# Batch 2's input stage partly by seven block products, with sums moved between VectorE and GpSimd and a reordered lead-in and last tile

## The chip, the cores and the metric

The kernel runs on one core of a Trainium2 chip. A core has TensorE (PE, matrix products), VectorE (DVE), ScalarE (ACT), GpSimd (POOL) and SyncE (SP), which run side by side and wait for one another through semaphores. SBUF is the memory on the core, PSUM the eight banks that PE writes its products to. The metric is the device time of one execution in microseconds (us). Times are medians of several runs; a profile is one profiled execution, whose time is a little different.

## The reference

Sparse attention over four batches, eight heads, 768 positions of 64 values, followed by a feed-forward layer. Each query sees the keys within 15 positions, and a summary of each block of 32 keys: the maximum of the block's keys, and the mean of its values, with log(32) added to the score.

```python
k_sum = k.reshape(B, H, nb, block, D).max(axis=3)
v_sum = v.reshape(B, H, nb, block, D).mean(axis=3)
scores_l = where(abs(pos_q - pos_k) < 16, scale * q @ k.T, -1e9)
scores_s = scale * q @ k_sum.T + np.log(32)
a = softmax(concat(scores_l, scores_s))
x = (a @ concat(v, v_sum)).transpose(0, 2, 1, 3).reshape(3072, 512)
h = x @ w_in                                 # 512 -> 2048
g = h * (1.0 / (1.0 + np.exp(-1.702 * h)))   # gelu
out = g @ w_out                              # 2048 -> 512
```

## The kernel before, in words

**Stages.** The four batches run one behind the other, each with an input stage (x times w_in, then the gelu on ACT into `gT`) and an output stage (gT times w_out). Attention of batch b+1 runs in small pieces beside batch b's output stage. A lead-in (0 to about 20.5 us in the trace) makes the attention of batch 0's first half before anything else can run; there `idle(n)` issues n matmuls of no use that keep PE busy. Batch 2's input stage lies at 120.9 to 142.4 us, its output stage at 142.4 to 164.9, batch 3's input stage at 164.9 to 183 and its output stage to 202.4.

**Order.** There is no scheduler: every engine executes its instructions in the order in which the program issues them (`_Ordered`), so an instruction that waits holds up all behind it on its engine. Pieces of attention are put between the products by tables: `plan` maps a slot (the number of the product behind which they come) to pieces: `s` scores of a head pair (PE, then the exponential on ACT), `m` masks (DVE, `a_sb` times `mk`), `v` values (PE into `ps_av`, then on DVE the reciprocal `rc` and the norm), `d` the transposing DMA into x, `g` the loading of the gelu's table. The two digits are the half of the batch and the index; m12, for instance, is the mask of half 1, head pair 2, and v10 the values of half 1, first group.

**Input stage.** w_in has 16 tiles of 128 columns and a batch two halves of 384 rows. Plainly, each tile and half takes four matmuls of 384 columns (tile `ph`), then a gelu. Tiles j and j+8 make a pair. From batch 1 on, the output stage uses seven block products in place of eight (in the manner of Strassen), which needs sums of gelu outputs, `gs`, made by `g_sums(j)` for each pair, four sums each. Batch 3's input stage does the same for six of its eight pairs: `ff_product(j, n)` is product n of pair j, two matmuls each; 14 matmuls for a pair instead of 16. It needs sums of w_in's quarters, `wsi` (`win_sum(0..3)`, each an operation of 128 x 2048 on DVE, at the start of batch 2's input stage), and sums of x, `xs` (`x_sums`). Between the products of a pair stand copies of partial results: "a" (DVE, bank A to bank C), "s" (ACT, bank E to SBUF), "b" (DVE, A plus s into B), "c" (DVE, A plus s into E), and gelus from the banks C, B, E and A. `steps` gives the slot of each. For this the PSUM banks are divided into A (3), B (1), C (2) and E (2) by `last_bank`. In the other stages PSUM is a pool of four single banks (`pmm`, tag mm) and one of two double banks (`psb`, tag big).

**Beside the input stages** the keys and values of the batch after next are prepared: `value_rows` sums each block of v on PE (`vsum`, tile `ps_vs`), adds the two halves on DVE (`block_sums`: a copy to `vpart`, then four adds to `vs`) and spreads them by DMA; `rest_k` takes the block maxima of the keys (a reduction on DVE to `ks`) and copies them to their places in `kx`.

**Output stage.** For each row tile t of three, seven products of eight matmuls of 256 columns (`product(b, t, what)`, banks poA, poB, poC), in the order of `seq`; outputs are put together on DVE (`osb` = bank plus s1, s2 or s5) and by ACT, and are stored from SP's queue.

In the profile every instruction has line 28, that of the helper which keeps the order; instructions are told apart by their tiles. The names of tiles are kept when their memory is used again: the weight sums appear as writes to `kx` and `qT`, the x sums as writes to `vw`.

Of the kernel before, what the change touches and what calls it, by code (L numbers as in the profile page):

```python
# [9 lines left out]
F32 = mybir.dt.float32  # L10
# [25 lines left out]
def kernel(  # L36
# [308 lines left out]

    def flat_kx(p, s):
        return kx[p][s].rearrange("p t c -> p (t c)")

    def key_rows(p, s, ks, eng=dve, j0=0):
        flat = flat_kx(p, s)  # L350
# [225 lines left out]
                     in_=qb2[g].rearrange("p i a h d -> p (i a h d)"), transpose=True)  # L576

    def rest_k(p, s, eng=dve):
        ks = attp.tile([128, nb], BF16, name="ks", tag="ks")
# [21 lines left out]
    def values(b, half, g):  # L601
# [7 lines left out]
        for i in range(2):  # L609
# [4 lines left out]
            for hh in range(2):  # L614
                for j in range(JH):
                    for e in range(2):
# [2 lines left out]
                                  rhs=vw[b % 2][:, half * TH + t, p + hh * NP if b else 2 * p + hh, 0:D + 1],  # L619
                                  start=True, stop=True, skip_group_check=True)  # L620
        x2[g] = attp.tile([128, 2, JH, 2, D], F16, name="x2", tag="x2", bufs=4)
        for i in range(2):
            norm(x2[g][:, :, :, i].rearrange("p h j d -> p j h d") if b else x2[g][:, i], pvs[i])

    def norm(x, pv):
        rc = attp.tile([128, 2, JH, 1], F32, name="rc", tag="rc")
# [53 lines left out]
        gelu(half, nt, ph)  # L680


    def g_sums(j, eng=dve, which=(0, 1, 2, 3)):

        a1, a2 = gTb[:, j], gTb[:, j + NT // 2]
        l, r = slice(0, HALF), slice(HALF, S)
        for w in which:
            a, b_, op = {0: (a1[:, r], a2[:, r], ALU.add), 1: (gs[:, 0, j], a1[:, l], ALU.subtract),
                         2: (a1[:, l], a1[:, r], ALU.subtract), 3: (a2[:, l], gs[:, 1, j], ALU.subtract)}[w]
            eng.tensor_tensor(out=gs[:, w, j], in0=a, in1=b_, op=op)  # L690

    N1 = d_model // 2

# [22 lines left out]
    def win_sum(what):  # L716
# [6 lines left out]
        dve.tensor_tensor(out=wsi[what], in0=a, in1=b_, op=op)  # L723

    def x_sums():

# [3 lines left out]

    plast = {}

    def last_bank(tag, name):
        return plast[tag in "AB"].tile([128, 512], F32, name=name, tag="last" + tag,
                                       bufs={"A": 3, "E": 2, "B": 1, "C": 2}[tag])

    ff_now = {}

# [36 lines left out]
    def product(b, t, what):  # L775
# [30 lines left out]
        def give(o, cols, name):  # L806
# [4 lines left out]
            else:  # L811
                act.activation(out=now[t, o][:, cols], in_=po, func=ACT.Copy)

        def store(o, tok, cols=slice(0, d_model)):
            r0 = b * S + tok
            sp.dma_start(out=out[r0:r0 + 128, cols], in_=now[t, o][:, cols])
            if cols.start == 0:
                now.pop((t, o))

        last = b == B - 1 and t == JH - 1  # L820

        if what == 1:
            keep_it("s1")
        elif what == 2:
            give("o1", lo, "s1")
        elif what == 6:
            keep_it("s2")
        elif what == 5:
            keep_it("s5")
        elif what == 7:  # L830
            give("o2", hi, "s5")
            if last:
                store("o2", HALF + t * 128, hi)
        elif what == 3:
            give("o1", hi, "s2")
            store("o1", t * 128)
        else:
            give("o2", lo, None)
            store("o2", HALF + t * 128, lo if last else slice(0, d_model))

    seq = [(0, 1)]
    for t in range(JH):
# [129 lines left out]
    av_blocks(1)  # L972
    v_norm(0)
# [139 lines left out]


    halves[0] = True
    for b in range(1, B - 1):
        nxt = b + 1 < B
        s = (b + 1) % 2
        if b == B - 2:
            for w in range(4):  # L1120
                win_sum(w)
        for n in range(0, NT, 2):
            if n == 0:
                ff_open(order2[0:4], (lambda: tx(1, 1)) if b == 1 else None)
            elif n == 2:
                for nt in order2[0:4]:
                    ff_one(1, nt)
                g_sums(0)
                g_sums(1)
            else:  # L1130
                for nt in order2[n:n + 2]:
                    for half in range(2):
                        ff_one(half, nt)
                g_sums(n // 2, dve, (0, 1) if n + 2 == NT else (0, 1, 2, 3))
            if nxt:
                if n == 0 and b > 1:
                    pool.tensor_copy(out=gate2, in_=xTT[1][1][:, 1, 0:1])
                    load_turned(q, b + 1, qb2, "qb")
                if n // 2 == 1:
                    value_rows(s)  # L1140
                if n // 2 == 2 * b:
                    xq(0, s)
                    xq(1, s)
                if n // 2 in (2, 3, 4, 5):
                    rest_k(n // 2 - 2, s)
        if nxt:
            exp_soon()
            beside(b + 1, -1)
        i = 0
        for t, what in seq:  # L1150
            product(b, t, what)
            if i == 0:
                g_sums(NT // 2 - 1, dve, (2, 3))
            if nxt:
                beside(b + 1, i)
            i += 1
            if nxt and b + 2 < B:
# [6 lines left out]
    for ab in (True, False):  # L1164
        plast[ab] = ctx.enter_context(tc.tile_pool(name=f"plast{ab:d}", bufs=2, space=bass.MemoryType.PSUM))
    b, n = B - 1, NT // 2
    PLAIN = 2

    def plain(nt, half, tag):
        ph = last_bank(tag, "ph")[:, 0:HALF]  # L1170
        ff_step(ph, half, nt)
        gelu(half, nt, ph)

    def ff_do(j, what):
        if isinstance(what, int):
            ff_product(j, what)
        elif what in "asbc":
            ff_copy(j, what)
        elif what == "g":
            g_sums(j, pool, (0, 1))  # L1180
        else:
            ff_gelu(j, what)

    for i, tag in enumerate("CCEEAAA"):
        plain((0, n, 1, n + 1)[i % 4], i // 4, tag)
# [1 line left out]
            x_sums()  # L1187
        if i in (5, 6):
            g_sums(0, pool, (0, 1) if i == 5 else (2, 3))
    steps = {0: [1, "a"], 1: [5, "s"], 9: [7, "c"], 10: [3], 4: [2], 5: [6, "b"], 13: [4],  # L1190
             6: ["C"], 11: ["B"], 12: ["E"], 14: ["A"], 15: ["g"]}
    for slot in range(7 * (n - PLAIN)):
        if slot == 1:
            plain(n + 1, 1, "B")
# [14 lines left out]
    ff_do(n - 1, 4)  # L1209
    ff_do(n - 1, "A")  # L1210
    product(b, 2, 1)
    q_ = slice(PLAIN, n)
    dve.tensor_tensor(out=gs[:, 2, q_], in0=gTb[:, q_, 0:HALF], in1=gTb[:, q_, HALF:S], op=ALU.subtract)
    dve.tensor_tensor(out=gs[:, 3, q_], in0=gTb[:, PLAIN + n:2 * n, 0:HALF], in1=gs[:, 1, q_], op=ALU.subtract)
    for t, what in seq:
        if what != 1:
            product(b, t, what)


# [28 lines left out]
```

## Time and profile before

| | |
|---|---|
| median of 3 runs | 206.34 us (206.1 to 206.46) |
| the profiled execution | 207.68 us |
| its span in the trace | 205.9 us |
| PE busy | 199.3 us, 97% of the span |
| DVE busy | 140.8 us, 68% |
| ACT busy | 125.2 us, 61% |
| GpSimd (POOL) busy | 92.1 us, 45% |
| chain that ended last | PE 89%, DMA 5%, DVE 3%, ACT 1% |

The span is the time from the first to the last record; the profiled execution's own time holds 1.8 us more around it. A line of a timeline reads: start, duration, engine, line, operation, output<-inputs with partitions x elements, count, and in brackets the idle time ahead of it with what ended it. The starts are counted from the span's beginning. Where several instructions are in one line, the duration runs from the first one's start to the last one's end; matmuls follow each other faster than each one's own duration.

### The profile page before, as it was taken

The page shows a single profiled execution, that of the slowest core. Times are in us where ns is not written, and L with a number is a line of the kernel's source. Part 1 is how long each engine was busy: PE and PEld are TensorE (multiplying, and loading weights), DVE is VectorE, ACT ScalarE, POOL GpSimd, SP SyncE. Part 2 cuts the span into 40 slices and gives each one's busy share as a digit, 9 for nine tenths or more (in the row PEclk, how much of TensorE's full clock was granted, in tenths as well). Part 3 has the DMA queues.
Part 4 walks back from the last instruction along what each step waited for, and adds up shares of the span by engine and source line. Part 5 has one row for each costly group of instructions (what it writes and reads, how often), then busy time and mean ns, then how long its engine had stood idle before and what let it go on. Part 6 is the DMA issues. An engine that isn't in the chain of part 4 may idle for free.

```text
span 205.9 us, 5854 instructions
## 1 busy us (share of the span) xinstructions
PE 199.3 (97%) x2360; PEld 138.5 (67%) x2360; DVE 140.8 (68%) x388; ACT 125.2 (61%) x239; POOL 92.1 (45%) x143
## 2 busy tenths in 40 slices
PE   6999999999999999999999999999999999999992
PEld 6668564556754466656888875666888865678882
DVE  6495796594856693899667789896769536758221
ACT  4474975728886726677772446778670577984220
POOL 7974589457999690006970035000000009991000
PEclk9999999999999999999999999999999999999999
DMA  6999999999999999999996979999022640000222
GB/s 174 170 167 205 208 207 207 189 154 243 147 99 162 183 163 171 167 150 159 147 144 87 138 168 127 124 251 172 0 105 73 151 135 3 0 0 3 102 103 102
DMA packets 95850, 28.13 MB, mean 137 GB/s; under 512 B 83648, under 2 KB 92880, under 8 KB 95824
## 3 DMA queue, kind: packets, MB, share of 16 engines
q0 software_dynamic: 69648, 13.24, 80.5%
q1 hardware_dynamic: 26176, 14.52, 33.2%
q8 instruction: 18, 0.29, 0.6%
q14 instruction: 8, 0.07, 0.1%
HBM read 27.26 MB, written 6.29 MB: 163 GB/s over the span
## 4 chain that ended last, share of the span: by engine, by line
PE 89%; DMA 5%; DVE 3%; ACT 1%; issue 0%; SPq 0%; DVEq 0%
PE ph L28 33%; PE poA L28 16%; PE poB L28 8%; PE po L28 8%; PE ps_av L28 4%; PE poC L28 4%; PE phA L28 4%; PE ps_s L28 4%; DMA vw<-vs 3%; DMA gT<-in_k_dram 2%; PE ps_x L28 1%; PE ps_k L28 1%; PE ps_t L28 1%; PE phB L28 1%; PE phC L28 1%; PE ps_q L28 1%
## 5 line engine op out<-in xcount | busy, mean ns | idle before, releaser
L28 PE MATMUL ph<-xT,w_in_sb 128*128 128x384 f16 x416 | 70.2, 326 | 0.1
L28 PEld LDWEIGHTS <-w_in_sb 128*128 128x128 f16 x452 | 43.7, 98 | 27.8 <-issue 0.2
L28 ACT ACTIVATE gT<-ph 128x384 f16<-128x384 f32 x104 | 49.8, 491 | 18.6 <-PE ph L28 18.2
L28 PEld LDWEIGHTS <-gT 128*128 128x128 f16 x312 | 28.8, 98 | 11.0
L28 ACT ACTIVATE a_sb<-ps_s 128x768 bf16<-128x768 f32 (+1 forms) x32 | 25.0, 826 | 12.7 <-PE ps_s L28 12.7
L28 PEld LDWEIGHTS <-gs 128*128 128x128 f16 x288 | 27.7, 98 | 3.4
L28 POOL DMA_DIRECT2D vw<-in_v_dram x36 | 24.6, 705 | 9.4 <-DMA kb<-in_k_dram 4.7
L28 POOL TENSOR_TENSOR gs<-gT 128x384 f16<-128x384 f16 x9 | 8.2, 908 | 43.1 <-ACT gT L28 43.1
L28 PE MATMUL po<-w_out_sb,gT 128*128 128x512 f16 x96 | 23.6, 380 | 0.0
L28 DVE TENSOR_TENSOR a_sb<-a_sb,mk 128x768 bf16<-128x768 bf16 x28 | 14.9, 555 | 6.5 <-ACT a_sb L28 5.9
L28 PE MATMUL poA<-ws,gs 128*128 128x256 f16 x144 | 18.7, 273 | 0.0
L28 DVE TENSOR_TENSOR x<-ps_av,rc 128x384 f16<-128x384 f32 x32 | 17.8, 558 | 1.1
L28 DVE TENSOR_TENSOR gs<-gT 128x384 f16<-128x384 f16 (+1 forms) x34 | 13.3, 393 | 6.9 <-ACT gT L28 6.6
L28 POOL DMA_DIRECT2D qb<-in_q_dram x16 | 15.1, 970 | 3.2 <-DMA v0n<-in_v_dram 1.7
L28 PEld LDWEIGHTS <-kx 64*128 64x128 bf16 (+1 forms) x372 | 9.4, 95 | 6.8 <-issue 4.0
L28 POOL DMA_DIRECT2D kb<-in_k_dram x14 | 13.6, 985 | 0.3 <-issue 0.3
L28 DVE TENSOR_REDUCE ks<-kx 128x24 bf16<-128x768 bf16 x12 | 11.4, 948 | 3.3 <-ACT kx L28 3.0
L28 ACT ACT_TABLE_LOAD x10 | 12.8, 1283 | 1.0 <-PEq L1232 0.8
L28 ACT ACTIVATE osb<-poA 128x256 f32<-128x256 f32 x9 | 3.5, 384 | 15.8 <-PE poA L28 15.8
L28 ACT ACTIVATE s<-poA 128x256 f32<-128x256 f32 x11 | 4.2, 385 | 11.2 <-PE poA L28 11.2
L28 PEld LDWEIGHTS <-a_sb 128*64 128x64 bf16 (+2 forms) x400 | 7.9, 108 | 3.2 <-issue 1.7
L28 PE MATMUL poA<-w_out_sb,gT 128*128 128x256 f16 x72 | 9.4, 273 | 0.0
(117 smaller groups left out, 287.7 us busy)
## 6 DMA issues: line engine op xcount, KB each, us to landing
out_dram<-osb SPq DMA_DIRECT2D x23, 256.0 KB, 3.4
kb<-in_k_dram POOLq DMA_DIRECT2D x14, 192.0 KB, 6.3
qb<-in_q_dram POOLq DMA_DIRECT2D x12, 192.0 KB, 9.4
vw<-in_v_dram POOLq DMA_DIRECT2D x36, 64.0 KB, 5.2
w_out_sb<-in_moe_w_out_dram POOLq DMA_DIRECT2D x4, 512.0 KB, 12.6
w_in_sb<-in_moe_w_in_dram POOLq DMA_DIRECT2D x3, 512.0 KB, 12.5
vw<-vs SPq DMA_DIRECT2D x6, 198.0 KB, 6.7
gT<-in_k_dram SPq DMA_DIRECT2D x2, 384.0 KB, 3.5
```

Of the source, the lines that this page charges most:

```text
L28: r = f(*a, **kw)
```

## The change

1. **Batch 2's input stage** becomes `in_seven(b, 4)`: pairs 0 to 3 plainly, pairs 4 to 7 by seven products each, in PSUM banks of the A, B, C, E division. The pools `pmm` and `psb` are closed before it and opened anew behind it. `vsum` puts its block sums into two banks of tag E there. The first product of the second seven-product pair (j = 5) comes in another slot than `steps` has it.
2. **Weight sums.** `win_sum(0)` and `win_sum(2)` run on GpSimd behind products 8 and 9 of batch 1's output stage, `win_sum(1)` and `win_sum(3)` on DVE behind products 17 and 19. None is left at the start of batch 2's input stage.
3. **Sums of gelu outputs.** The sums are merged over two pairs where that goes. In batch 2, sums 2 and 3 of pairs 0 and 1, and sums 0 and 1 of pairs 4 to 6, run on GpSimd; sums 2 and 3 of pairs 2 to 7 are two large DVE operations (128 x 2304) behind products 0 and 1 of its output stage, where the scores that came first are put behind the first product.
4. **Keys and norms.** `rest_k2` does two head pairs at once; the copies to `kx` run on GpSimd in batch 2. The norm of a values step is one reciprocal and one product from batch 2's values on.
5. **Lead-in.** Eight idle matmuls more at the start and fewer later, `s_bias(1)` ahead of the turns of q, two copies of q on ACT in place of DVE, and the block scores of the second group (`b_turn(1)`, `b_exp(1)`) behind `av_edges`.
6. **Last row tile.** Order 6, 5, 7, 2, 3, 4 instead of 5, 6, 2, 7, 3, 4; the first output is stored in two halves, and the last 256 columns are copied half by DVE and half by ACT and stored from two queues.

```diff
     def vsum(s):
-        if s == 1 and not vs_ps[0]:
+        if plast:
+            ps = [last_bank("E", "ps_vs") for e in range(2)]
+        elif s == 1 and not vs_ps[0]:
...
+    def rest_k2(g, s, eng=dve):
+        flat = kxs[s].rearrange("p i t c -> p (i t c)")
+        o, n = 2 * g * NQ * 128, 2 * NJ
+        ks = attp.tile([128, 2, nb], BF16, name="ks", tag="ks2", bufs=2)
+        dve.tensor_reduce(out=ks.rearrange("p i (j e n) -> p (i j) e n", e=2, n=2),
+                          in_=at(flat, o, [[256, n], [192, 2], [block, 2], [1, block]]),
+                          axis=AX.X, op=ALU.max)
+        eng.tensor_copy(...)
...
+        if b > 1:
+            rc = attp.tile([128, 2, 2 * JH, 1], F32, name="rc", tag="rc2", bufs=2)
+            dve.reciprocal(out=rc, in_=pv[..., D:D + 1])
+            dve.tensor_mul(x2[g].rearrange("p h j i d -> p i (h j) d"), pv[..., 0:D],
+                           rc.to_broadcast([128, 2, 2 * JH, D]))
+            return
...
...
+        elif last:
+            for c, eng, queue in ((slice(0, 128), dve, sp), (slice(128, N1), act, act)):
+                copy(eng, now[t, "o2"][:, c], po[:, c])
+                queue.dma_start(...)
...
-    idle(28)
+    idle(36)
     k_turn(0)
     k_own(0, act)
     s_bias(0)
-    idle(4)
+    idle(2)
     k_turn(1)
     k_own(1, act)
+    s_bias(1)
     q_turn(0)
     q_turn(1)
-    s_bias(1)
     q_copy(0, dve)
-    q_copy(1, dve)
+    q_copy(1, act)
     k_max(0)
-    idle(8)
+    idle(6)
...
-    q_copy(3, dve)
+    q_copy(3, act)
...
-    b_turn(1)
-    b_exp(1)
...
     av_edges(1)
+    b_turn(1)
+    b_exp(1)
...
+    def in_seven(b, first):
+        n, s = NT // 2, (b + 1) % 2
+        pool.tensor_copy(out=gate2, in_=xTT[1][1][:, 1, 0:1])
+        load_turned(q, b + 1, qb2, "qb")
+        for i, tag in enumerate("CCEEAAAB"):
+            plain((0, n, 1, n + 1)[i % 4], i // 4, tag)
+            if i == 3:
+                x_sums()
+        g_sums(0, dve, (0, 1), 2)
+        value_rows(s)
+        for i, tag in enumerate("EEAA"):
+            plain(2 + n * (i % 2), i // 2, tag)
+        rest_k2(0, s, pool)
+        g_sums(2, dve, (0, 1))
+        for i in range(2):
+            plain(3 + n * i, 0, "E")
+        g_sums(0, pool, (2, 3), 2)
+        for slot in range(7 * (n - first)):
+            for j in range(first, n):
+                at_ = slot - 7 * (j - first)
+                if j == first + 1 and at_ in (0, -5):
+                    at_ = -1 if at_ == 0 else 0
+                for what in steps.get(at_, ()):
+                    ff_do(j, what)
+            if slot == 8:
+                xq(0, s)
+                xq(1, s)
+            if slot == 10:
+                rest_k2(1, s, pool)
+        last = n - 1
+        ff_do(last - 1, "A")
+        plain(3, 1, "C")
+        ff_do(last, 7)
+        ff_do(last, "c")
+        ff_do(last, 3)
+        ff_do(last - 1, "g")
+        ff_do(last, "B")
+        ff_do(last, "E")
+        plain(3 + n, 1, "E")
+        ff_do(last, 4)
+        ff_do(last, "A")
+        g_sums(last, dve, (0, 1))
+        g_sums(3, dve, (0, 1))
...
-        if b == B - 2:
-            for w in range(4):
-                win_sum(w)
...
         for t, what in seq:
             product(b, t, what)
+            if seven and i < 2:
+                next(bulk)
             if i == 0:
-                g_sums(NT // 2 - 1, dve, (2, 3))
+                if seven:
+                    beside(b + 1, -1)
+                else:
+                    g_sums(NT // 2 - 1, dve, (2, 3))
+            beside(b + 1, i)
             i += 1
...
+                if i in (9, 10):
+                    win_sum(2 * (i - 9), pool)
+                if i in (18, 20):
+                    win_sum(i - 17)
...
-    for t, what in seq:
-        if what != 1:
+    for t in range(JH):
+        for what in (5, 6, 2, 7, 3, 4) if t + 1 < JH else (6, 5, 7, 2, 3, 4):
             product(b, t, what)
```

More of the change, by code (lines that the diff above doesn't have):

```diff
@@ L722, in win_sum @@
                      2: (a11, a21, ALU.subtract), 3: (a12, wsi[1], ALU.subtract)}[what]
[L723 removed]
+        eng.tensor_tensor(out=wsi[what], in0=a, in1=b_, op=op)
     def x_sums():
@@ L731, with open_last, plain, ff_do @@
     plast = {}
+    def open_last(stack, b):
+        for tag, n in (("A", 3), ("B", 1), ("C", 2), ("E", 2)):
+            plast[tag] = stack.enter_context(tc.tile_pool(name=f"last{tag}{b}", bufs=n, space=bass.MemoryType.PSUM))
     def last_bank(tag, name):
-        return plast[tag in "AB"].tile([128, 512], F32, name=name, tag="last" + tag,
-                                       bufs={"A": 3, "E": 2, "B": 1, "C": 2}[tag])
+        return plast[tag].tile([128, 512], F32, name=name, tag="last" + tag)
+    def plain(nt, half, tag):
+        ph = last_bank(tag, "ph")[:, 0:HALF]
+        ff_step(ph, half, nt)
+        gelu(half, nt, ph)
+    def ff_do(j, what):
+        if isinstance(what, int):
+            ff_product(j, what)
+        elif what in "asbc":
+            ff_copy(j, what)
+        elif what == "g":
+            g_sums(j, pool, (0, 1))
+        else:
+            ff_gelu(j, what)
+    steps = {0: [1, "a"], 1: [5, "s"], 9: [7, "c"], 10: [3], 4: [2], 5: [6, "b"], 13: [4],
+             6: ["C"], 11: ["B"], 12: ["E"], 14: ["A"], 15: ["g"]}
     ff_now = {}
@@ L812, in give @@
                 act.activation(out=now[t, o][:, cols], in_=po, func=ACT.Copy)
+        last = b == B - 1 and t == JH - 1
         def store(o, tok, cols=slice(0, d_model)):
@@ L816, in store @@
             sp.dma_start(out=out[r0:r0 + 128, cols], in_=now[t, o][:, cols])
-            if cols.start == 0:
+            if not last:
                 now.pop((t, o))
-        last = b == B - 1 and t == JH - 1
         if what == 1:
@@ L825, in product @@
             give("o1", lo, "s1")
+            if last:
+                store("o1", t * 128, lo)
         elif what == 6:
@@ L835, in product @@
             give("o1", hi, "s2")
-            store("o1", t * 128)
+            store("o1", t * 128, hi if last else slice(0, d_model))
+        elif last:
+            for c, eng, queue in ((slice(0, 128), dve, sp), (slice(128, N1), act, act)):
+                copy(eng, now[t, "o2"][:, c], po[:, c])
+                queue.dma_start(out=out[b * S + HALF + t * 128:b * S + HALF + t * 128 + 128, c],
+                                in_=now[t, "o2"][:, c])
         else:
             give("o2", lo, None)
-            store("o2", HALF + t * 128, lo if last else slice(0, d_model))
+            store("o2", HALF + t * 128)
     seq = [(0, 1)]
@@ new lines @@
+    for b in range(1, B - 1):
+        seven = b == B - 2
+        if seven:
+            mid.close()
+            with ExitStack() as banks:
+                open_last(banks, b)
+                in_seven(b, 4)
+            plast.clear()
+            mid = ExitStack()
+            pmm = mid.enter_context(tc.tile_pool(name="pmm2", bufs=4, space=bass.MemoryType.PSUM))
+            psb = mid.enter_context(tc.tile_pool(name="psb2", bufs=2, space=bass.MemoryType.PSUM))
+            bulk = sums23(2)
+        else:
+            in_plain()
+        exp_soon()
+        if not seven:
@@ L1161 @@
                     xk(i // 2 - 8, b % 2)
+                if i in (9, 10):
+                    win_sum(2 * (i - 9), pool)
+                if i in (18, 20):
+                    win_sum(i - 17)
     mid.close()
-    for ab in (True, False):
-        plast[ab] = ctx.enter_context(tc.tile_pool(name=f"plast{ab:d}", bufs=2, space=bass.MemoryType.PSUM))
+    open_last(ctx, B - 1)
     b, n = B - 1, NT // 2
     PLAIN = 2
[L1169 to L1182, printed above, removed]
     for i, tag in enumerate("CCEEAAA"):
```

80 lines of the change are left out of this document (44 added, 36 removed).

## The prediction

> **What bounds the kernel now.** I read the busy shares and the chain on the page first, then the busy time by stage, then the timelines of each engine around the places that the change touches.
>
> ```profile
> PE 199.3 (97%) x2360; PEld 138.5 (67%) x2360; DVE 140.8 (68%) x388; ACT 125.2 (61%) x239; POOL 92.1 (45%) x143
> PE 89%; DMA 5%; DVE 3%; ACT 1%; issue 0%; SPq 0%; DVEq 0%
> ```
>
> ```profile
> 0.00:20.50 20.50, 18.24 (x334) 14.14 (x334) 13.03 (x44) 10.95 (x17) 14.80 (x23) 1.00 1.43 179
> ...
> 98.40:120.90 22.50, 22.50 (x361) 19.34 (x358) 15.78 (x41) 12.14 (x21) 8.53 (x14) 1.00 1.33 142
> 120.90:142.40 21.50, 21.50 (x185) 12.82 (x184) 19.59 (x57) 15.24 (x33) 4.41 (x5) 1.00 1.52 161
> ...
> 164.90:183.00 18.10, 18.04 (x113) 10.78 (x111) 11.16 (x21) 14.99 (x35) 13.16 (x15) 1.00 0.13 38
> ```
>
> In the second view the columns behind the stretch and its length are PE, PEld, DVE, ACT and POOL. PE has no gap in batch 1's output stage (98.40 to 120.90) or batch 2's input stage (120.90 to 142.40), so there a matmul saved is time saved and every new wait of PE is time lost. In batch 2's input stage DVE is the next engine, 19.59 of 21.50. Batch 3's input stage (164.90) already works by seven products and loses 0.06. Idle PE is left in the lead-in (2.26) and at the end.
>
> **The change, term by term.** Minus is time won.
>
> *Matmuls.*
>
> ```profile
> 170.61 0.49 PE L28 MATMUL phC<-xT,w_in_sb 128*128 128x384 f16 x2
> 170.94 0.49 PE L28 MATMUL phA<-vw,kx 128*128 128x384 f16 x2
> ...
> 171.59 0.49 PE L28 MATMUL phE<-vw,kx 128*128 128x384 f16 x2
> 172.14 0.48 PE L28 MATMUL phA<-vw,kx 128*128 128x384 f16 x2
> ```
>
> A tile pair takes 16 matmuls plainly and 14 by seven products; four pairs save 8. In the first two rows two matmuls follow two others by 0.325 us (170.61 to 170.94), 0.1625 each, so 8 x 0.1625 = −1.3.
>
> *Lead-in.*
>
> ```profile
> 1.30 3.17 PE L28 MATMUL ps_h<-warm 128*128 128x128 bf16 x28 [1.30 <-DVE warm L28]
> 4.96 0.85 PE L28 MATMUL ps_k<-wide,kb 128*64 128x128 bf16 x12 [0.49 <-ACT kb L28]
> ...
> 7.08 0.85 PE L28 MATMUL ps_k<-wide,kb 128*64 128x128 bf16 x12
> ...
> 11.15 0.53 PE L28 MATMUL ps_k<-wide,kb 128*64 128x128 bf16 x12
> ...
> 15.59 0.34 PE L28 MATMUL ps_b<-qT,ks 64*32 64x384 bf16 x2 [0.39 <-DVE ks L28]
> ```
>
> ```profile
> 11.21 1.83 ACT L28 ACTIVATE a_sb<-ps_s 128x960 bf16<-128x960 f32 x2 [2.42 <-PE ps_s L28]
> ...
> 14.44 1.83 ACT L28 ACTIVATE a_sb<-ps_s 128x960 bf16<-128x960 f32 x2 [0.32 <-PE ps_s L28]
> ```
>
> The same 12 transposes take 0.85 at 7.08 and 0.53 at 11.15: PE turns fast only at about 10.7, 5.75 behind the end of its only gap, 4.47 to 4.96, though the clock column reads 1.00. Eight idle matmuls more (3.17/28 = 0.11 each, 0.9) cover that gap of 0.49. Counted from 1.30, fast then comes at about 7.1; the first transposes start 0.2 later, what follows runs at double speed, and the first exponentials (11.21) start some 1.7 earlier. The second two (14.44) gain only about 1.2: the copy of q pair 3 now stands on ACT behind both first ones and two other ACT operations. The 0.39 at 15.59 goes, since that step now stands behind other matmuls. I take −1.4; −1.8 if all follows PE, +0.4 if fast does not come sooner (0.2 later start and a longer ACT queue), −0.2 if only the stall goes. The Trainium skill ("TensorE: Matmul & The Clock Gate", Part 1) says that the full clock follows some 3.4 us of busy time in a free-running window; by that it would come between 4.7 and 8.1 and the term would be about the same. The 5.75 measured behind the gap is within two such windows.
>
> *Weight sums: GpSimd, and the masks beside them.*
>
> ```profile
> 52.47 0.68 DVE L28 TENSOR_TENSOR ws<-w_out_sb 128x1024 f16<-128x1024 f16 x1
> ...
> 55.22 0.83 DVE L28 TENSOR_TENSOR ws<-w_out_sb,ws 128x1024 f16<-128x1024 f16 x1
> ...
> 108.20 1.26 DVE L28 TENSOR_TENSOR a_sb<-a_sb,mk 128x768 bf16<-128x768 bf16 x2 [1.05 <-ACT a_sb L28]
> ...
> 119.27 0.42 DVE L28 TENSOR_TENSOR osb<-poA,s 128x256 f32<-128x256 f32 x1 [0.45 <-PE poA L28]
> ...
> 120.50 1.22 DVE L28 TENSOR_TENSOR kx<-w_in_sb 128x2048 f16<-128x2048 f16 x1
> ...
> 185.49 0.68 DVE L28 TENSOR_TENSOR gs<-gT 128x384 f16<-128x384 f16 x1 [0.66 <-ACT gT L28]
> 186.20 0.36 DVE L28 TENSOR_TENSOR gs<-gs,gT 128x384 f16<-128x384 f16 x1
> 186.48 1.35 DVE L28 TENSOR_TENSOR gs<-gT 128x2304 f16<-128x2304 f16 x1
> ```
>
> ```profile
> 55.45 0.89 POOL L28 COPY kx<-ks 128x288 bf16<-128x288 bf16 x1
> ...
> 104.23 3.40 POOL L28 DMA_DIRECT2D vw<-in_v_dram  x5 [0.30 <-DMA vw<-in_v_dram]
> ...
> 185.04 0.91 POOL L28 TENSOR_TENSOR gs<-gs,gT 128x384 f16<-128x384 f16 x1
> ```
>
> ```profile
> 113.75 0.95 PE L28 MATMUL ps_av<-vw,a_sb 128*64 128x65 bf16 x48
> ```
>
> GpSimd is free for sums 0 and 2 behind its last load (104.23 + 3.40 = 107.63). One takes at most 2048/384 x 0.91 = 4.85. Masks m12 and m13 (DVE, 108.20) fall into the first. That DVE is then held is seen at 185.49: an operation that takes 0.36 alone takes 0.68, ending when the GpSimd sum of 185.04 has ended. So m12 and m13 run at about 112.5 to 113.8 instead of 108.2 to 109.5; behind them in DVE's queue stand the output of poC, two reciprocals and norms (0.2 and 0.56 each in pairs), and PE's values step v10 at 113.75 waits for the PSUM bank of v00 (+0.9), v11 for that of v01 (+0.6): +1.5. Not held at all is 0. The other bound: the second mask gets in only behind sum 2, DVE is free at 117.6, and v10 waits 5.4: +6.0. At 55.22 a DVE sum got in between two GpSimd copies and took 0.83 instead of 0.68, so DVE goes between two operations; I take +1.5. The Trainium skill ("SBUF — State Buffer", Who interferes with whom) says that a DVE instruction with two SBUF inputs and a GpSimd one that reads SBUF exclude each other for a whole instruction; the 185.49 row agrees for 0.9 us, and no row shows it for 4.85. By that rule alone the term is +1.5 or +6.0, never 0.
>
> Sum 1 (1.22 on DVE) now stands ahead of the poA output of 119.27, which the second-last product's bank waits for: +0.3 (0 to 0.6).
>
> *Block sums of v in two E banks.* Before they had a bank of the score pool.
>
> ```profile
> 120.92 5.20 PE ph L28 x32
> 126.12 0.53 PE ps_vs L28 x48
> ```
>
> ```profile
> 127.89 0.28 DVE L28 COPY vpart<-ps_vs 128x128 f32<-128x128 f32 x1
> 128.21 1.18 DVE L28 TENSOR_TENSOR vs<-ps_vs,vpart 32x128 bf16<-32x128 f32 x4
> ...
> 131.13 0.94 DVE L28 TENSOR_REDUCE ks<-kx 128x24 bf16<-128x768 bf16 x1
> ...
> 164.86 0.56 DVE L28 TENSOR_TENSOR vw<-xT,xT 128x768 f16<-128x768 f16 x1 [0.27 <-DMA xT<-x]
> ...
> 171.52 0.57 DVE L28 TENSOR_TENSOR phB<-phA,vw 128x384 f32<-128x384 f32 x1 [1.04 <-PE phA L28]
> ```
>
> From the stage's start PE is done with eight plain halves and the block sums at 5.20 + 0.53 = 5.73. The next two plain halves need those E banks. DVE first does two sums of gelu outputs (0.55 each, as at 164.86) that need the eighth gelu, whose end is about 5.7, then the copy (0.28): 7.1, a wait of 1.4. The second E bank comes with the four adds (1.18): 0.57 more. +2.0 (1.4 to 2.6, the adds' full length at the upper end).
>
> *First seven-product pair (4).*
>
> ```profile
> 126.16 0.49 ACT L28 ACTIVATE gT<-ph 128x384 f16<-128x384 f32 x1 [0.16 <-PE ph L28]
> ```
>
> With 0.57 for each DVE step (171.52), product 2 waits about 0.24 for step a, and product 7 about 0.55 for step b, since only one product lies between 6 and 7 where batch 3 has two (there the 172.14 row still came 0.22 late: 0.55 behind a pair of matmuls that takes 0.325): +0.8 (0.2 to 1.2). Beside it the first merged sums on DVE meet the merged GpSimd sums of pairs 0 and 1 (768 wide, 2 x 0.91), by the rule of the 185.49 row: +0.9 (0 to 2.4).
>
> *Second key maximum.* Two 0.94 reductions merge to about 1.7, and it stands on DVE between step c of pair 4 and step b of pair 5; PE's product 7 of pair 5 waits: +1.1 (0 if the keys land late enough to fall between pairs, 1.4).
>
> *End of the stage.* The first product of tile 2's output needs bank A that the last pair's gelu (0.49) frees, and DVE's bulk sums (1.35 each, as at 186.48) now stand ahead of the copy of s2, which product 7 of tile 0 waits for: +1.0 and +0.4, +1.4 (0.6 to 2.0). Before, neither stood there.
>
> *Tail.*
>
> ```profile
> 202.38 0.38 ACT L28 ACTIVATE osb<-poA 128x256 f32<-128x256 f32 x1 [3.11 <-PE poA L28]
> ```
>
> The last copy is halved between DVE and ACT (an estimate of about 0.28 for half the columns of the 0.38) and stored from two queues: −0.15 (−0.4 to +0.2, a later queue).
>
> *At no cost:* merged norms, merged key rows and sums in batch 1 and the key copies on GpSimd lie beside a dense PE in DVE's and GpSimd's free time (15.78 of 22.50 and 4.41 of 21.50); uncovered, the merged norm would delay a values step by about 0.5. The key copies that move to GpSimd stand there ahead of the merged sums and behind the loads of q for batch 3; the scores that need them come after the stage's end, so a few us of delay are covered. The last tile's new order keeps its products and only adds a store to SP's queue and one to ACT's, both while earlier stores run.
>
> Sum: −1.3 − 1.4 + 1.5 + 0.3 + 2.0 + 0.8 + 0.9 + 1.1 + 1.4 − 0.15 = +5.15. The profiled execution took 207.68 (span 205.9), 1.34 over the median of the runs: 212.8 for it, 211.5 for the median.
>
> **Rivals.** *Both GpSimd sums hold the masks:* +6.0 in place of +1.5: 206.34 + 9.65 = 216.0. For it: the two sums follow each other without a gap. Against: 55.22.
> *GpSimd holds nothing:* the +1.5 and +0.9 fall, +2.75, 209.1. For it: the 120.50 operation has no neighbour that would show it. Against: 185.49.
> *Faster: DVE keeps the banks in time.* One mechanism: DVE, rid of 4.9 of weight sums in the stage, runs ahead of PE as in batch 3's (0.06 idle of 18.10), so only the copy's 1.4 and 0.2 at the first pair remain: −1.3 − 1.4 + 0.3 + 1.4 + 0.2 − 0.15 = −0.95, 205.4. It decides once PE's new waits in all (the three stages together) stay under 2.85. Against: the E banks' wait is the order of DVE's queue, and DVE keeps two reductions that batch 3's stage lacks.
>
> **How the numbers follow.** Forecast 0.40 (its own range 210 to 213), both sums held 0.20, nothing held 0.25, faster 0.12, no change 0.03. Less than 0.41 (0.2%) can't be told from none here. Faster 0.12, same 0.03, slower 0.85. The range 206.6 to 217.0 leaves out the faster case and the highest end.
>
> **What the profile after would show.** The 12 key transposes at 7.2 take 0.53; masks m12 and m13 start behind 112; a PE gap of about 1.4 behind the ps_vs group and one of 0.55 at the first product 7; a wait at the first product of tile 2. Wrong if PE stays dense from 98 to 143, or if GpSimd's sums take much less than 4.85, or if the transposes at 7.2 still take 0.85.

## The result and the profile after

| | before | after |
|---|---|---|
| median of 5 runs | 206.34 us (206.1 to 206.93) | 213.49 us (212.71 to 213.88) |
| the profiled execution | 207.68 us | 213.49 us |
| its span | 205.9 us | 211.8 us |
| PE busy | 199.3 us (97%) | 199.6 us (94%) |

The ratio is 1.0334 with a 95% interval of 1.0304 to 1.0365: slower. The medians differ by 7.15 us, the profiled executions by 5.81. The page after:

```profile
span 211.8 us, 5822 instructions
...
PE 199.6 (94%) x2356; PEld 137.6 (65%) x2356; DVE 136.3 (64%) x325; ACT 127.1 (60%) x245; POOL 111.9 (53%) x163
...
PEclk9999999999999999999999996999999999999999
```

PE does fewer matmuls and is yet busy for 0.3 us longer, and one slice of 40, that from about 127 to 132 us, has a clock of 0.6. Three rows of PE in the trace of before are the marks against which the ledger below is measured: the first product of batch 1's output stage, the start of batch 2's input stage and the last product.

```profile
98.75 1.05 PE L28 MATMUL poA<-w_out_sb,gT 128*128 128x256 f16 x8
...
120.76 5.36 PE L28 MATMUL ph<-xT,w_in_sb 128*128 128x384 f16 x32
...
201.30 1.04 PE L28 MATMUL poA<-ws,gT 128*128 128x256 f16 x8
```

PE's timeline after, first the lead-in and the start of batch 1's output stage, then batch 2's input stage:

```profile
6.66 0.53 PE L28 MATMUL ps_k<-wide,kb 128*64 128x128 bf16 x12
...
97.52 1.05 PE L28 MATMUL poA<-w_out_sb,gT 128*128 128x256 f16 x8
...
112.52 0.95 PE L28 MATMUL ps_av<-vw,a_sb 128*64 128x65 bf16 x48
...
119.46 1.03 PE L28 MATMUL poA<-ws,gT 128*128 128x256 f16 x8 [0.64 <-DVE osb L28]
120.33 5.36 PE L28 MATMUL ph<-xT,w_in_sb 128*128 128x384 f16 x32
125.62 0.60 PE L28 MATMUL ps_vs<-vw,E 64*32 64x128 bf16 x48
127.66 0.81 PE L28 MATMUL ph<-xT,w_in_sb 128*128 128x384 f16 x4 [1.43 <-DVE vpart L28]
128.87 5.08 PE L28 MATMUL ph<-xT,w_in_sb 128*128 128x384 f16 x20 [0.41 <-DVE vs L28]
133.79 0.49 PE L28 MATMUL phA<-xT,w_in_sb 128*128 128x384 f16 x2
...
134.44 0.49 PE L28 MATMUL phA<-xT,w_in_sb 128*128 128x384 f16 x2
135.92 0.48 PE L28 MATMUL phC<-xT,w_in_sb 128*128 128x384 f16 x2 [0.99 <-DVE phC L28]
...
136.57 0.49 PE L28 MATMUL phE<-vw,kx 128*128 128x384 f16 x2
137.44 0.48 PE L28 MATMUL phA<-vw,kx 128*128 128x384 f16 x2 [0.39 <-DVE phB L28]
...
139.39 0.49 PE L28 MATMUL phE<-vw,kx 128*128 128x384 f16 x2
140.71 0.48 PE L28 MATMUL phA<-vw,kx 128*128 128x384 f16 x2 [0.83 <-DVE phB L28]
...
146.56 0.49 PE L28 MATMUL phA<-vw,w_in_sb 128*128 128x384 f16 x2
147.80 1.03 PE L28 MATMUL poA<-w_out_sb,gT 128*128 128x256 f16 x8 [0.75 <-ACT gT L28]
...
151.94 0.52 PE L28 MATMUL ps_s<-qT,kx 64*128 64x64 bf16 x24
152.61 1.03 PE L28 MATMUL poA<-ws,gs 128*128 128x256 f16 x8
...
207.11 1.04 PE L28 MATMUL poA<-ws,gT 128*128 128x256 f16 x8
```

A wait costs more than the idle time in brackets, since the matmul behind it no longer overlaps the one ahead; the loss is read from start to start. Two matmuls of 384 columns need 0.325. From 134.44 to 135.92, for example, 1.48 - 0.325 = 1.16 are lost. The group at 128.87 holds 20 matmuls that need 3.25 and take 4.92 to the start at 133.79: 1.67 lost with no wait in it. The busy time by stretches (the third number from the right is the granted clock) tells why:

```profile
128.00:129.00 1.00, 0.59 (x4) 0.28 (x3) 0.94 (x4) 0.49 (x1) 0.00 (x0) 0.94 2.54 145
129.00:130.00 1.00, 1.00 (x4) 0.44 (x3) 1.00 (x1) 0.00 (x0) 0.00 (x0) 0.50 1.66 97
...
132.00:133.00 1.00, 1.00 (x7) 0.56 (x6) 0.00 (x0) 0.43 (x2) 1.00 (x1) 0.85 1.18 256
```

Right behind the two waits for the E banks the clock is halved for some 3.4 us (0.94 in the stretch to 129, 0.50 from 129 to 132, 0.85 in the stretch to 133). The ledger against the trace of before (the value for a wait is the distance from one start to the next, less what the matmuls or transposes between them need without a wait):

| step | predicted | in the traces, start to start |
|---|---|---|
| saved matmuls | -1.3 | -1.3 (by count) |
| lead-in | -1.4 | -1.23 (first product of batch 1's output: 98.75 to 97.52) |
| masks held by GpSimd | +1.5 | 0 (PE dense to 118.6) |
| sum 1 ahead of the poA output | +0.3 | +0.80 (the shift falls from -1.23 to -0.43 at the stage's start, 120.76 to 120.33) |
| E banks | +2.0 | +2.06 (1.50 and 0.56) |
| half clock | none | +1.67 |
| first pair with the held sums | +1.7 | +1.70 (1.16 and 0.55) |
| second key maximum | +1.1 | +1.00 |
| end of the stage | +1.4 | +1.13 (0.92 and 0.21) |
| tail | -0.15 | +0.09 (last product to the end: 4.60 to 4.69) |
| sum | +5.15 | +5.92 (span +5.9, own time +5.81) |

DVE and GpSimd after, around the masks and the first pair:

```profile
106.97 1.26 DVE L28 TENSOR_TENSOR a_sb<-a_sb,mk 128x768 bf16<-128x768 bf16 x2 [1.05 <-ACT a_sb L28]
...
117.50 1.56 DVE L28 TENSOR_TENSOR kx<-kx,w_in_sb 128x2048 f16<-128x2048 f16 x1
...
133.21 1.67 DVE L28 TENSOR_TENSOR gs<-gT 128x384 f16<-128x384 f16 x1 [2.61 <-ACT gT L28]
...
138.44 1.74 DVE L28 TENSOR_REDUCE ks<-kx 128x48 bf16<-128x1536 bf16 x1
```

```profile
106.49 3.39 POOL L28 DMA_DIRECT2D vw<-in_v_dram  x5 [0.56 <-PE ps_s L28]
109.85 8.13 POOL L28 TENSOR_TENSOR kx<-w_in_sb 128x2048 f16<-128x2048 f16 x2
...
133.03 1.62 POOL L28 TENSOR_TENSOR gs<-gT,gs 128x768 f16<-128x768 f16 x1
```

GpSimd's loads came later than in the trace of before (106.49 instead of 104.23), so its weight sums (8.13 for the two) began behind the masks. Where the two did meet, DVE was held: sum 1 took 1.56 instead of 1.22, and the sum at 133.21 took 1.67 instead of 0.36. The ledger compares one execution with one other, and it says where time was lost, not what the time would fall by if one row went: the half clock's row is such a case, as the first experiment shows.

### The profile page after: what moved, and what is told of

The parts are those of the page before. It is cut to its first block, busy times and chain, and to the rows that moved or that the text cites. A ratio compares the mean times of both kernels' runs of the same rounds, so it can differ in the third digit from the quotient of the medians.

```text
span 211.8 us, 5822 instructions
## 1 busy us (share of the span) xinstructions
PE 199.6 (94%) x2356; PEld 137.6 (65%) x2356; DVE 136.3 (64%) x325; ACT 127.1 (60%) x245; POOL 111.9 (53%) x163
## 5 line engine op out<-in xcount | busy, mean ns | idle before, releaser
L28 PE MATMUL ph<-xT,w_in_sb 128*128 128x384 f16 x352 | 62.0, 332 | 1.9 <-DVE vpart L28 1.4
L28 PEld LDWEIGHTS <-w_in_sb 128*128 128x128 f16 x412 | 40.3, 99 | 29.5 <-issue 5.3
L28 ACT ACTIVATE gT<-ph 128x384 f16<-128x384 f32 x88 | 42.3, 491 | 19.1 <-PE ph L28 18.5
L28 POOL TENSOR_TENSOR gs<-gT 128x384 f16<-128x384 f16 (+1 forms) x13 | 12.6, 966 | 28.6 <-ACT gT L28 28.5
L28 DVE TENSOR_TENSOR gs<-gT 128x384 f16<-128x384 f16 (+2 forms) x17 | 11.0, 649 | 13.7 <-ACT gT L28 13.7
L28 PEld LDWEIGHTS <-kx 64*128 64x128 bf16 (+1 forms) x396 | 11.7, 95 | 9.8 <-issue 5.9
L28 DVE TENSOR_TENSOR x<-ps_av,rc 128x384 f16<-128x384 f32 (+1 forms) x24 | 16.6, 691 | 0.8
L28 ACT ACTIVATE osb<-poA 128x256 f32<-128x256 f32 (+1 forms) x9 | 3.3, 372 | 17.0 <-PE poA L28 13.5
L28 DVE TENSOR_REDUCE ks<-kx 128x24 bf16<-128x768 bf16 (+1 forms) x8 | 10.8, 1350 | 3.5 <-ACT kx L28 3.2
L28 PE MATMUL phA<-vw,kx 128*128 128x384 f16 x40 | 9.8, 325 | 1.3 <-DVE phB L28 1.2
```

Of the source, the lines that this page charges most:

```text
L28: r = f(*a, **kw)
```

## The experiments

**Filling the waits for the E banks.** Is the half clock a consequence of the waits? `fill(n)` issues n matmuls of 384 columns, of no use, into a spare A bank.

```diff
         value_rows(s)
+        fill(10)
         for i, tag in enumerate("EEAA"):
             plain(2 + n * (i % 2), i // 2, tag)
+            if i == 0:
+                fill(3)
```

> The changed kernel with 10 matmuls of no use on PE behind the block sums of v and 3 behind the next plain half, into a spare A bank: they fill the two waits of 1.43 and 0.41 us. In the changed kernel PE runs at a granted clock of 0.50 from 129 to 132 us, right behind these waits; the 20 matmuls there take 5.08 us instead of some 3.3. Theory (the waits cause the half clock): the clock stays at 1.00 and the time falls by about 2.2, to 211.3. Rival (the half clock has another cause, such as the point in time or the load): it drops all the same and the time is 213.5 to 213.8.

Measured: 214.25 us (213.69 to 214.76); ratio to before 1.0371, 1.0335 to 1.0408. No gain, but the half clock had moved. PE's timeline and the stretches of this kernel:

```profile
129.53 3.41 PE L28 MATMUL ph<-xT,w_in_sb 128*128 128x384 f16 x20
...
136.23 0.73 PE L28 MATMUL phC<-xT,w_in_sb 128*128 128x384 f16 x2 [2.31 <-DVE phC L28]
136.76 0.85 PE L28 MATMUL phA<-vw,kx 128*128 128x384 f16 x2
137.40 0.85 PE L28 MATMUL phE<-vw,kx 128*128 128x384 f16 x2
```

```profile
136.00:138.00 2.00, 1.77 (x6) 0.85 (x6) 0.94 (x3) 0.49 (x1) 0.46 (x2) 0.58 1.20 182
```

```profile
133.91 1.67 DVE L28 TENSOR_TENSOR gs<-gs,gT 128x384 f16<-128x384 f16 x1
```

The 20 matmuls take 3.41 again, at full clock. But PE arrives earlier at the first seven-product pair, while DVE's two sums there are now both held by GpSimd, 1.67 each: a wait of 2.31 in place of 0.99, and behind it two matmuls take 0.64 at a clock of 0.58. So in these traces the half clock follows the wait, and the time won was lost at the next place. The second DVE sum takes 1.31 more than in the changed kernel (1.67 instead of 0.36), because it now meets GpSimd's second sum; that alone eats most of the 1.67 that the full clock gives back.

The times say the same. The clock over the whole execution is recorded for each run: 3.4 us at half in 211.8 would leave about 0.992. Two of the five executions of the changed kernel have 1.00 (213.56 and 213.46 us), and two of the four of this one 0.997 and 1.00 (213.69 and 213.84). As far as that record goes, without a half clock of that length none of them is faster than the median of the changed kernel by more than 0.03, though the two runs of this one that have it are some 0.9 slower than the two that do not. The waits thus do not halve the clock in every execution, and the half clock is not what makes the changed kernel slow; where those executions lost the time was not traced.

**The block sums first on DVE.**

```diff
-        g_sums(0, dve, (0, 1), 2)
         value_rows(s)
+        g_sums(0, dve, (0, 1), 2)
```

> The changed kernel with the copy and the four adds of the block sums of v ahead of the first two sums of gelu outputs in DVE's order. The E bank comes free at about 126.5 instead of 127.7: the first wait falls from 1.43 to 0.3, the second is 0.5 to 0.6 (the adds' 1.18 behind it). Theory (order on DVE makes the wait, and the wait makes the half clock): no half clock, -0.9 and -2.2, 210.3. Rival (the wait shrinks but the clock drops still): 212.5. Rival (the wait is of another cause): 213.5.

Measured: 210.58 us (209.15 to 210.89), ratio 1.0181, 1.0141 to 1.0221, as the theory has it. The trace is of the fastest run, 209.15, which had already started batch 2's input stage 0.65 earlier than the changed kernel (119.68 for 120.33). PE's timeline, then a row of DVE:

```profile
125.98 0.81 PE L28 MATMUL ph<-xT,w_in_sb 128*128 128x384 f16 x4 [0.40 <-DVE vpart L28]
127.19 3.41 PE L28 MATMUL ph<-xT,w_in_sb 128*128 128x384 f16 x20 [0.41 <-DVE vs L28]
```

```profile
129.90 0.35 DVE L28 TENSOR_TENSOR gs<-gT 128x384 f16<-128x384 f16 x1
```

Behind waits of 0.40 and 0.41 the clock stays at 1.00 here. DVE's sums at the first pair now run ahead of GpSimd's (the first takes 0.35 instead of 1.67), so that wait shrinks as well. From the start of the input stage to the first product of the output stage PE gains 3.69 on the changed kernel in the two traces: 1.04 at the E banks, 1.67 of the half clock and 0.98 at the first pair. One edit takes all three, so their shares come from the traces and not from the times.

**The lead-in alone**, in the kernel before.

```diff
-    idle(28)
+    idle(36)
...
-    idle(4)
+    idle(2)
...
+    s_bias(1)
     q_turn(0)
     q_turn(1)
-    s_bias(1)
...
-    q_copy(1, dve)
+    q_copy(1, act)
...
-    idle(8)
+    idle(6)
...
-    q_copy(3, dve)
+    q_copy(3, act)
...
-    b_turn(1)
-    b_exp(1)
...
     av_edges(1)
+    b_turn(1)
+    b_exp(1)
```

> The kernel before with the lead-in alone changed. In the two traces the lead-in part moves the start of batch 1's output stage from 98.75 to 97.52, -1.23. Theory (all of it is kept to the end): 206.34 falls to 205.1. Rival (the profiled execution of before, 1.34 above its median, had an unlucky start that the other executions did not have, since the moment at which PE turns fast differs between executions): the median falls by 0 to 0.4 only, 205.9 to 206.3.

Measured: 206.81 us (205.76 to 207.71, 12 runs), beside 206.26 of before (205.53 to 207.84, 17 runs); ratio 1.0006, 0.998 to 1.0033: the rival, in that the median does not fall. Its trace has the early full speed (the 12 transposes at 6.66 take 0.53), and a second trace of the kernel before has it nearly as early:

**The kernel before once more.**

> The kernel before once more, for a second trace of its lead-in. If the moment at which PE turns fast differs between executions of one kernel, the 12 transposes at 7.08 take 0.53 in this one, or the time from 4.96 to the first full-speed group is other than 5.75, and the first product of batch 1's output stage starts up to 1.3 us from 98.75, in step with the time. If the start is the same in each execution, it starts within 0.1 of 98.75 and the times differ by something behind it.

```profile
4.85 0.85 PE L28 MATMUL ps_k<-wide,kb 128*64 128x128 bf16 x12 [0.38 <-ACT kb L28]
...
6.97 0.59 PE L28 MATMUL ps_k<-wide,kb 128*64 128x128 bf16 x12
...
97.57 1.05 PE L28 MATMUL poA<-w_out_sb,gT 128*128 128x256 f16 x8
```

This execution took 206.5. With the old lead-in PE turned fast at about 7 instead of 10.7, the first product came at 97.57 instead of 98.75, and the time is lower by the same 1.18. So the late start in the first trace of before is not in every execution of that kernel; that execution's 1.34 above the median and the 1.4 that the prediction credits to the lead-in are for the most part one and the same thing. Nor is it a single accident: the trace of the weight sums alone, further down, has the old lead-in too, and there the transposes at 7.21 take 0.85 and the first product comes at 98.61. The seven traces with the new lead-in are all fast by 6.93, yet their first products lie anywhere from 96.19 to 98.30, so the start of that product scatters by other causes too. What takes up the gain of the early start in the median is not shown.

**The masks one slot later**, so that they meet GpSimd's sums.

```diff
+            if b == 1 and i == 10:
+                for m in (2, 3):
+                    mask(1, m)
+            if not (b == 1 and i == 9):
-            beside(b + 1, i)
+                beside(b + 1, i)
```

> The changed kernel with masks m12 and m13 of batch 2's attention one slot later, at about 109.45, so that they meet GpSimd's first weight sum (109.85 to 113.9 in the changed kernel, where the masks had ended before it began). Theory (a DVE operation with two SBUF inputs waits for the whole GpSimd operation): the second mask ends at about 114.5, values step v10 waits some 3 us, time +3 to +4 (217); up to +7.5 if it waits for both sums. Rival (GpSimd does not hold DVE for so long): the masks take 1.0 together and the time is within 0.3 of 213.5.

Measured: 223.59 us (222.67 to 224.51), ratio 1.0813, 1.0764 to 1.0862: 10.1 over the changed kernel, more than the 7.5 expected at most. DVE, GpSimd and PE:

```profile
110.21 9.78 DVE L28 TENSOR_TENSOR a_sb<-a_sb,mk 128x768 bf16<-128x768 bf16 x2
```

```profile
110.98 8.11 POOL L28 TENSOR_TENSOR kx<-w_in_sb 128x2048 f16<-128x2048 f16 x2
```

```profile
121.18 0.87 PE L28 MATMUL ps_av<-vw,a_sb 128*64 128x65 bf16 x24 [7.80 <-DVE x L28]
```

Two masks, 0.56 each when free, take 9.78, the first of them 9.31: DVE is held through both sums and does not get in between the two. By the records the mask at 110.21 even started 0.77 ahead of the first sum. PE waits 7.80, and its clock is 0.50 from about 116 until about 126, which the expectation did not count.

**The weight sums alone**, in the kernel before.

```diff
...
-        if b == B - 2:
-            for w in range(4):
-                win_sum(w)
...
+                if i in (9, 10):
+                    win_sum(2 * (i - 9), pool)
+                if i in (18, 20):
+                    win_sum(i - 17)
```

> The kernel before with the weight sums alone moved as in the change: sums 0 and 2 on GpSimd behind products 8 and 9 of batch 1's output stage, sums 1 and 3 on DVE behind products 17 and 19. In the trace of before GpSimd's loads end at 107.63 and masks m12 and m13 start at 108.20, so GpSimd is first. Theory (both sums hold the masks, as they did for 9.78 us when the masks came one slot later): the second mask ends at about 116.5, values steps v10 and v11 wait 4 to 7 us and PE's clock halves for some time behind: 211 to 217. Rival (the loads end later than the masks here too, as in the changed kernel, where the sums began at 109.85): 206.3 to 207, with a wait of 0.8 at the second-last product.

Measured: 216.27 us as the median of four runs (210.18, 215.6, 216.94 and 217.41), beside 207.15 of before. These runs scatter too far for an interval; the shortest is 3.0 over before. The trace is of the run of 215.6:

```profile
108.76 9.16 DVE L28 TENSOR_TENSOR a_sb<-a_sb,mk 128x768 bf16<-128x768 bf16 x1
```

```profile
109.39 8.10 POOL L28 TENSOR_TENSOR kx<-w_in_sb 128x2048 f16<-128x2048 f16 x2
```

```profile
119.70 0.87 PE L28 MATMUL ps_av<-vw,a_sb 128*64 128x65 bf16 x24 [6.01 <-DVE x L28]
```

Here the first mask passed and the second was held from 108.76 to 117.92, 0.43 past the end of the sums. In this execution, this part of the change alone moves the start of batch 2's input stage from 120.76 to 129.16, by 8.40: the rival of the prediction in which both sums hold the masks. Why one run of the four lost only 3.0 was not traced, so the price of this part alone is open between 3.0 and 10.3 us. In the traced execution of the whole change it did not come to that, since the masks had ended 1.62 before the sums began.

**All waits of the changed kernel taken away at once** (called e6 below).

```diff
+        rest_k2(0, s, pool)
+        g_sums(0, pool, (0, 1), 2)
         value_rows(s)
-        for i, tag in enumerate("EEAA"):
+        for i, tag in enumerate("AAEE"):
             plain(2 + n * (i % 2), i // 2, tag)
-        rest_k2(0, s, pool)
-        g_sums(2, dve, (0, 1))
-        for i in range(2):
-            plain(3 + n * i, 0, "E")
+        rest_k2(1, s, pool)
+        g_sums(2, pool, (0, 1))
+        plain(3, 0, "E")
         g_sums(0, pool, (2, 3), 2)
...
+            if slot == 1:
+                plain(3 + n, 0, "E")
...
-            if slot == 10:
-                rest_k2(1, s, pool)
...
-            if seven and i < 2:
+            if seven and i in (0, 2):
                 next(bulk)
...
-                if i in (18, 20):
-                    win_sum(i - 17)
+                if i == 20:
+                    win_sum(1)
+                    win_sum(3)
```

Product 1 of pair 5 is back in its usual slot, and the scores stand ahead of the first product of batch 2's output stage.

> The changed kernel with its waits taken away one by one: the first key maximum ahead of the block sums of v and the second behind them, before the seven-product pairs; sums 0 and 1 of pairs 0 to 2 on GpSimd; the next plain halves in banks A, A, E, E; a plain half between products 1 and 5 of pair 4, and product 1 of pair 5 in its usual slot; weight sums 1 and 3 behind the last output of batch 1; the scores ahead of the first product of batch 2's output stage and the second bulk sum behind the copy of s2. By the ledger of the changed kernel, start to start: the bank waits (1.5 and 0.6), the half clock (1.7), the first pair (1.7, of which 0.2 to 0.4 stays), the key maximum (1.0), the end of the stage (1.1, of which 0.3 stays) and the poA output (0.8) go: 213.5 - 7.7 = 205.8 with the eight matmuls saved. Rival (DVE's or GpSimd's work in the stage is too much in any order, so the waits move on to other places): 208 to 210.

Measured: 212.44 us (210.16 to 213.07), before 207.15; ratio 1.025, 1.0212 to 1.0289. That is neither the 205.8 expected nor the 208 to 210 of its rival. The trace is of the fastest run, 210.16. DVE and PE:

```profile
130.39 1.75 DVE L28 TENSOR_REDUCE ks<-kx 128x48 bf16<-128x1536 bf16 x1 [4.73 <-DMA kx<-kb]
```

```profile
132.79 0.48 PE L28 MATMUL phC<-xT,w_in_sb 128*128 128x384 f16 x2 [3.94 <-DVE phC L28]
```

All the other waits went or shrank (none at the E banks and at the poA output), but the second key maximum, put ahead of step a, waited for its keys to land, and with it DVE's queue and PE; the clock was 0.50 again behind that (134 to 136). What the runs around 212.4 lost beyond this one is not seen in it.

**The second key maximum in four parts**, behind step c of each seven-product pair, in the kernel just shown. Each `next(parts)` issues one of four reductions of a quarter each, and the last one the copies.

```diff
-        rest_k2(1, s, pool)
         g_sums(2, pool, (0, 1))
+        parts = key_parts(1, s, pool)
...
+            if slot in (9, 16, 23):
+                next(parts)
...
         ff_do(last, "c")
+        next(parts)
...
         ff_do(last - 1, "g")
+        next(parts)
```

> The kernel of e6 with the second key maximum cut into four reductions of about 0.5 us behind step c of pairs 4 to 7, where DVE has some 0.5 free in each pair; in e6 it stood ahead of step a of pair 4 and waited until 130.35 for the keys to land, and PE waited 3.94 for it and then ran at half clock. Theory (place on DVE and landing time of the keys make that wait, and the wait the half clock): both go, 3.94 + 0.16 + 1.7 less some 0.2 of new waits: 212.4 - 5.6 = 206.8, within 0.5 of the kernel before of the same call, since the 1.3 of the saved matmuls stand against waits of about 1 at the first pair and the end of the stage. Rival (DVE has no room for the reductions even in parts): waits of 0.4 at each of three pairs, 208.

Measured: 206.17 us (205.43 to 207.62, 12 runs) beside 207.04 of before (205.71 to 208.45, 17 runs); ratio 0.9967, 0.9938 to 0.9996. The waits of PE over its whole span, beyond the start:

```profile
PE ps_s L28 <- ACT qT L28: 0.6, 2, 0.4
PE ps_s L28 <- DVE qT L28: 0.6, 2, 0.4
PE ps_s L28 <- ACT gT L28: 0.4, 1, 0.4
```

Only the last lies in batch 2's stage (at its end); the clock is 1.00. With PE dense the whole loss is gone: the change with its waits removed is faster than the kernel before by 0.3%, as far as the interval goes. That fits the saved matmuls (1.3, less a few tenths of waits), but the other parts of the change are in this kernel too, so the 0.3% is not shown to be theirs alone.

## Why the prediction was right

The direction holds, and the time lies in the wide range (206.6 to 217.0), though above the 210 to 213 of the forecast itself. The mechanism holds: in a stage where PE has no gap the eight saved matmuls are worth 1.3 by count, and DVE's and ACT's hand-overs cost more. The E banks (2.06 for 2.0), the first pair with its held sums (1.70 for 1.7), the second key maximum (1.00 for 1.1) and the end of the stage (1.13 for 1.4) came as worked out, at the places named; the run with the block sums first takes the first of them down and the one with the parted key maximum takes nearly all of them away, and the time follows. That the trace came within 0.7 of 212.8 is in part luck: a term of 1.5 that did not come about was made up by 1.67 that the prediction did not have. The first pair's 1.70 is luck in its size too: with PE at full clock, as in the first experiment, the step a there alone loses 2.47.

Wrong in size or place:

- *Masks, +1.5.* The step that failed is the start of GpSimd's sums, taken as 107.63 from the trace of before. They began at 109.85, behind the masks. That DVE is held was right, but the value chosen was not: where they meet, DVE is held through both sums (9.31 and 9.16 for one mask), so the row at 55.22 misled. The prediction's "never 0" supposes that the two meet. They did not, and the price was nothing; where they met, it was above the upper bound of 6.0 (10.1 and, in one trace, 8.40). That DVE is held agrees with the exclusion that the Trainium skill states ("SBUF — State Buffer", Who interferes with whom), though the records do not show its order, by which the one that issues first goes first: the mask at 110.21 is recorded as starting 0.77 ahead of the sum, and GpSimd's recorded spans are rough. The start of GpSimd's sums is also no property of the change. In the second trace of the kernel before, the loads end at 108.96 (105.57 + 3.39) and the masks, which run from 107.02, at 108.28, so there too GpSimd is free only behind the masks. The order of the two differs between executions of one kernel, and the prediction read it from one.
- *No term for the clock, +1.67 in the trace.* The prediction knew half speed only in the lead-in and counted a wait as its own length. In the traced execution the clock was halved for 3.4 us behind a wait of 1.43 with another of 0.41 close to it. As the first experiment shows, the time does not fall by this 1.67 when the half clock is absent, since the first pair's wait then grows. The Trainium skill ("TensorE: Matmul & The Clock Gate", Part 1) gives half speed after at least one idle window of about 3.4 us. The half clock's length agrees; its condition does not, since here PE was idle for 1.84 of the 3.4 before it, and the measurement decides.
- *Sum 1, +0.3:* 0.80, of which 0.34 is the time that sum 1 was itself held, and its output queue with it.
- *Lead-in, -1.4, and the step to the median, -1.34.* The traces show -1.23, but the lead-in alone moves the median by nothing that can be measured. The late start of the traced execution was in the 1.34 as well as in the 1.4, so it was subtracted twice. Without the lead-in term the ledger gives 5.92 + 1.23 = 7.15 over the median of before, and the medians differ by 7.15. That the two agree to the last digit is chance, as the single traces scatter by more.

Of the rivals, that in which both sums hold the masks is real (the traces of the masks one slot later and of the weight sums alone) and was missed by the 1.62 us between two engines. That in which GpSimd holds nothing is refuted at 133.21 and by the same two traces. The faster one, DVE keeping the banks in time, needs other orders on DVE: the last experiment is that case, at 0.3%.

## What to carry to other kernels

In a stage where PE has no gap, price a saving of matmuls against every new hand-over from start to start, and reckon with a half clock behind waits like those here (1.84 idle in some 3.4), which come in some executions and not in others. A row of such a ledger is not yet a price: ask what the next hand-over would then wait for. Before one trace's slow start, or the order of two engines in it, is credited to a kernel, see whether the same kernel does so in other executions, and do not subtract the excess of that execution a second time. Work moved to GpSimd beside DVE operations with two SBUF inputs was free here where the two did not meet, and where they met it cost as much as 10.1, more than its own length of 8.13; which of the two hung on when GpSimd's loads were done.

## What the runs showed of the hardware that was not expected

- A PE idle for 1.84 of about 3.4 us ran at a granted clock of 0.50 for the next 3.4 (128.9 to 132.3); behind waits of 0.40 and 0.41 close together, and behind a single one of 0.99, it stayed at 1.00. In two of five executions of the same kernel the recorded clock over the whole run was 1.00, so by that record the same program does not always get the half clock.
- A DVE mask with two SBUF inputs, 0.56 alone, took 9.31 and 9.16 beside two GpSimd sums that followed each other (8.11 and 8.10 together), though it had started ahead of them by the records.
- The moment at which PE turned fast lay at about 7 in one execution of the kernel before and at 10.7 in another, while the clock column read 1.00 in both, so that column does not show half speed at the start.
